# Causal attention and a token/channel mixer on one core: the 64-key ends of probabilities times values as 64x64 tiles in two PSUM banks, with a new list of places

## The chip, the cores and the metric

The kernel runs on one core of a Trainium2 chip, in float32 throughout. The metric is the device time of one execution in microseconds, as the median over several runs; lower is better. PE is the matrix engine (TensorE), DVE VectorE, ACT ScalarE, POOL GpSimd, SP the engine that issues most DMAs. PSUM, which PE alone accumulates into, has eight banks of 512 float32 columns on 128 partitions.

## What is computed

Four batches of twelve heads of causal attention over 448 positions with 64 features a head; the heads' outputs side by side form x of 448 x 768. Then two two-layer networks with residuals: over the tokens (448 to 256 to 448) and over the channels (768 to 1536 to 768).

```python
scores = scale * np.matmul(q, k.transpose(0, 1, 3, 2))     # q, k, v: (4, 12, 448, 64)
scores = np.where(mask, -1000000000.0, scores)             # mask: key after query
scores = scores - np.max(scores, axis=-1, keepdims=True)
attn = np.exp(scores)
attn = attn / (np.sum(attn, axis=-1, keepdims=True) + 1e-09)
attn_out = np.matmul(attn, v)
x = attn_out.transpose(0, 2, 1, 3).reshape(B, S, H * D)
xt = x.transpose(0, 2, 1)
h = np.maximum(xt @ w_tok1, 0.0) @ w_tok2
u = x + h.transpose(0, 2, 1)
h2 = np.maximum(u @ w_ch1, 0.0) @ w_ch2
out = u + h2
```

The weights of both networks arrive as float64.

## The kernel before

The 48 heads are worked in 24 pairs, two heads side by side on the 128 partitions. For each pair `load_pair` fetches q, k and v (`blocks` for q and k, four DMAs each; `load` for v, three), `prep` transposes q and k on DVE, and `heads` computes scores, exponentials and sums in blocks of 64 queries. The scores are matmuls on 64x64 quarters of PE's array, so that both heads and two blocks run at once. The normalized probabilities are transposed, on PE for the first ten pairs (`by_tensor`) and by DMA for the others (`by_dma`), and `values` multiplies them with the values. `xturn` transposes the result for the token network (`tokens`), two pairs at a time; `split_u`, `channels` and `group` are the channel network, and `store` and `finish` write the output. Products of the networks are done as three products of rounded parts and remainders, on the whole 128x128 array.

The code makes jobs: a function that issues a few instructions on one engine, with the jobs it needs and the buffers and banks it holds. `Plan.job` gives each job its place from the table `PLACES` (by the job's name, its rank and a count) and, where several engines could do it, the engine from `CHOICE` ("a" ACT, "d" DVE, "p" POOL). `Plan.emit` then writes the instructions: at each planned moment each free engine takes, of the jobs whose needs are planned as done and whose banks are open, the one with the lowest place. The planned durations set this order alone; on the chip every engine executes its own queue in order and waits on semaphores. Where the plan finds PE without work in the first 75 us it puts a filler matmul there (`keep_warm`, line 861), into bank 7, which the other work gets only afterwards. `SHARE` limits how many banks a kind of work holds at once; `share("a")` is for `values`.

In `values` the 448 keys are summed in blocks of 128. With causality each block of 64 queries needs full 128-key blocks and, for every second one, an end of 64 keys. `SUMS` lists, as (value block, blocks of the transposed probabilities, first query block, number of query blocks), four products with full blocks and four ends of 64 queries. The ends too are 128 keys deep: a tile `vend` holds the values of the end in the half that counts and zeros in the other, which `load_pair.lower` and `load_pair.upper` copy there for every pair (line 635 is their copy, `[64x128]` and `[64x256]`), after a clearing at the start (line 874). One of the ends, the keys from 384 on, reads `vraw` itself, whose unused part is cleared. For each entry of `SUMS` there is a matmul for each of the two heads, on the left and the right 64 columns of the array (128x64 tiles), all into one bank, in two jobs (`range(2)`, `range(2, 8)`); line 1158 is the matmul. `evac` copies the 448 columns into `u` by one instruction.

Of the kernel before, what the change touches and what calls it, by code (L numbers as in the profile page):

```python
# [21 lines left out]
    "load_pair.blocks": {-2: (2, 3), 0: (4, 5), 2: (20, 10), 4: (52, 70), 6: (138, 160), 8: (213, 238), 10: (272,  # L22
# [3 lines left out]
    "load_pair.load": {0.5: (38,), 2.5: (94,), 4.5: (113,), 6.5: (193,), 8.5: (309,), 10.5: (322,), 12.5: (389,),  # L26
        14.5: (439,), 16.5: (463,), 18.5: (577,), 20.5: (606,), 22.5: (697,), 24.5: (764,), 26.5: (846,), 28.5:
        (951,), 30.5: (1021,), 32.5: (1107,), 34.5: (1216,), 36.5: (1255,), 38.5: (1443,), 40.5: (1403,), 42.5:
        (1539,), 44.5: (1564,), 46.5: (1642,)},
    "load_pair.lower": {-0.2: (67,), 1.8: (135,), 3.8: (143,), 5.8: (220,), 7.8: (354,), 9.8: (361,), 11.8: (434,),  # L30
        13.8: (476,), 15.8: (521,), 17.8: (600,), 19.8: (643,), 21.8: (732,), 23.8: (795,), 25.8: (872,), 27.8:
        (985,), 29.8: (1047,), 31.8: (1142,), 33.8: (1243,), 35.8: (1286,), 37.8: (1467,), 39.8: (1470,), 41.8:
        (1556,), 43.8: (1599,), 45.8: (1672,)},
    "load_pair.upper": {-0.2: (72,), 1.8: (139,), 3.8: (150,), 5.8: (234,), 7.8: (364,), 9.8: (371,), 11.8: (436,),
        13.8: (489,), 15.8: (528,), 17.8: (602,), 19.8: (645,), 21.8: (701,), 23.8: (798,), 25.8: (875,), 27.8:
        (987,), 29.8: (1054,), 31.8: (1152,), 33.8: (1246,), 35.8: (1291,), 37.8: (1468,), 39.8: (1481,), 41.8:
        (1559,), 43.8: (1612,), 45.8: (1678,)},
    "narrow.load": {3.5: (107, 128, 132, 176, 187, 205, 209, 233), 12: (305,), 13: (383,), 14: (450,), 15: (484,),
        16: (591,), 17: (666,), 18: (735,), 19: (791,), 20: (855,), 21: (916,), 22: (988,), 23: (1027,), 24:
        (1099,), 25: (1173,), 26: (1266,), 27: (1328,), 28: (1381,), 29: (1434,), 30: (1472,), 31: (1524,), 32:  # L40
        (1579,), 33: (1650,), 34: (1714,), 35: (1747,)},
    "narrow.size": {3.5: (146, 162, 178, 192, 215, 231, 247, 257), 12: (346,), 13: (429,), 14: (505,), 15: (572,),
        16: (635,), 17: (716,), 18: (763,), 19: (828,), 20: (893,), 21: (949,), 22: (1008,), 23: (1072,), 24:
        (1134,), 25: (1215,), 26: (1288,), 27: (1366,), 28: (1418,), 29: (1463,), 30: (1501,), 31: (1548,), 32:
        (1619,), 33: (1694,), 34: (1737,), 35: (1766,)},
    "narrow.shift": {3.5: (153, 170, 185, 207, 218, 236, 250, 266), 12: (357,), 13: (435,), 14: (511,), 15: (542,),
        16: (644,), 17: (722,), 18: (778,), 19: (834,), 20: (898,), 21: (962,), 22: (1013,), 23: (1076,), 24:
        (1140,), 25: (1237,), 26: (1298,), 27: (1370,), 28: (1426,), 29: (1458,), 30: (1509,), 31: (1551,), 32:
        (1623,), 33: (1698,), 34: (1741,), 35: (1771,)},
    "narrow.join": {3.5: (164, 177, 199, 210, 227, 242, 256, 274), 12: (363,), 13: (437,), 14: (524,), 15: (584,),  # L50
        16: (656,), 17: (729,), 18: (783,), 19: (845,), 20: (904,), 21: (970,), 22: (1019,), 23: (1081,), 24:
        (926,), 25: (1242,), 26: (1303,), 27: (1372,), 28: (1428,), 29: (1473,), 30: (1516,), 31: (1555,), 32:
        (1626,), 33: (1702,), 34: (1308,), 35: (1776,)},
    "token_weights.<lambda>": {3.5: (168, 181, 201, 216, 232, 245, 260, 273)},
    "token_weights.rest_of": {3.5: (171, 186, 204, 219, 244, 252, 267, 280)},
    "prep.turn": {-1.5: (1, 6), 0.5: (8, 19), 2.5: (56, 59), 4.5: (96, 109), 6.5: (180, 200), 8.5: (246, 269), 10.5:
# [4 lines left out]
    "heads.<lambda>": {0: (7, 9), 2: (25, 31), 4: (66, 75), 6: (114, 118), 8: (206, 212), 10: (279, 282), 12: (333,  # L61
# [473 lines left out]
def kernel(  # L535
# [17 lines left out]
    P = 128  # L553
# [585 lines left out]
    def values(g):  # L1139
# [720 lines left out]
```

## Time and profile before

| what | us |
|---|---|
| median of three runs | 550.89 |
| lowest and highest run | 549.56, 550.93 |
| the profiled execution, its own time | 550.41 |
| its span, first to last instruction | 548.6 |
| PE busy in the span | 538.4 |
| DVE, ACT, POOL busy | 432.7, 325.0, 151.0 |

The profile is of one execution. An engine's busy time is the time in which at least one of its instructions is under way; matmuls overlap one another, so the distance between two starts tells what one costs, and its duration does not. A float32 matmul of attention appears as two passes, two instructions each of one row. L1158 and the like are lines of the kernel before.

### The profile page before, as it was taken

How to read it: one execution, taken by the hardware profiler on the slowest of the kernel's cores; microseconds unless marked ns; L12 is line 12 of the kernel's file. 1: busy time of each engine (PE TensorE's matmuls, PEld its weight loads, DVE VectorE, ACT ScalarE, POOL GpSimd, SP SyncE). 2: the span in 40 equal slices, each digit the busy share in tenths (PEclk: the TensorE clock that was granted, in tenths of full speed). 3: DMA queues.
4: the chain of work that ended last, by engine and by line, in shares of the span. 5: the costliest groups of instructions: out<-in, count | busy, mean ns of one | idle time of the engine just before them, and what ended most of it. 6: DMA issues, size and time to landing. Idle time of an engine off the chain costs nothing.

```text
span 548.6 us, 11162 instructions
## 1 busy us (share of the span) xinstructions
PE 538.4 (98%) x3908; PEld 466.3 (85%) x3908; DVE 432.7 (79%) x1052; ACT 325.0 (59%) x764; POOL 151.0 (28%) x208
## 2 busy tenths in 40 slices
PE   8998999999999999999999999999999999999996
PEld 3677788888888888888888989999999999999995
DVE  5989888888878978988787897389897857484864
ACT  4989898888795979876768872154232313140300
POOL 2536542353332132122230265161200212100000
PEclk9999999999999999999999999999999999999999
DMA  6677778899899999998987664247632121212138
GB/s 114 135 166 151 155 185 216 199 157 197 204 186 189 191 193 196 186 195 200 206 168 197 149 146 158 67 115 154 135 86 77 40 86 33 72 41 86 30 64 138
DMA packets 231783, 77.68 MB, mean 142 GB/s; under 512 B 206000, under 2 KB 221232, under 8 KB 231728
## 3 DMA queue, kind: packets, MB, share of 16 engines
q1 hardware_dynamic: 220112, 75.37, 63.9%
q10 hardware_dynamic: 11616, 1.61, 1.8%
q8 instruction: 31, 0.51, 0.4%
q14 instruction: 24, 0.20, 0.1%
HBM read 49.15 MB, written 14.94 MB: 117 GB/s over the span
## 4 chain that ended last, share of the span: by engine, by line
PE 86%; DMA 6%; SPq 4%; DVE 1%; issue 1%; ACT 1%; POOL 0%; ACTq 0%; DVEq 0%
PE ps L1328 31%; PE ps L1747 14%; PE ps L1656 12%; PE ps L1158 6%; PE ps L971 6%; PE ps L1278 5%; PE ps L1245 4%; PE ps L1727 3%; SPq L889 3%; PE ps L1062 2%; DMA out_dram<-kq 2%; DMA vraw<-in_v_dram 2%; PE ps L1197 2%; DMA gl<-in_q_dram 1%; DMA wl<-in_moe_w_tok_dram 1%
## 5 line engine op out<-in xcount | busy, mean ns | idle before, releaser
L1395 DVE TENSOR_TENSOR u<-ps,u 128x448 f32<-128x448 f32 x118 | 73.1, 621 | 43.1 <-PE ps L1747 28.4
L1005 ACT ACTIVATE prob<-prob,stat 128x128 f32<-128x128 f32 (+6 forms) x168 | 83.6, 500 | 17.5 <-DVE stat L993 17.3
L993 DVE CUSTOM_DVE_ANT_0 prob<-ps,mask 128x256 f32<-128x256 f32 (+6 forms) x168 | 63.5, 416 | 7.5 <-PE ps L971 7.1
L1328 PE MATMUL ps<-uh,wh 128*128 128x448 f32 x144 | 54.4, 378 | 0.0
L633 ACT ACTIVATE wh<-wf 128x768 fp32r<-128x768 f32 x28 | 23.3, 842 | 52.4 <-PE ps L1747 33.1
L1328 PE MATMUL ps<-gh,wh 128*128 128x448 f32 x144 | 53.9, 374 | 0.0
L635 POOL TENSOR_SCALAR prob<-prob,stat 128x320 f32<-128x320 f32 (+6 forms) x70 | 38.2, 556 | 56.6 <-DVE stat L1027 42.9
L1328 PE MATMUL ps<-uh,wl 128*128 128x448 f32 x144 | 52.7, 366 | 0.5 <-DVE wl L644 0.5
L1328 PE MATMUL ps<-gh,wl 128*128 128x448 f32 x144 | 52.7, 366 | 0.0
L1328 PE MATMUL ps<-gl,wh 128*128 128x448 f32 x144 | 52.6, 365 | 0.0
L1328 PE MATMUL ps<-ul,wh 128*128 128x448 f32 x144 | 52.6, 365 | 0.0
L644 POOL TENSOR_TENSOR wl<-wf,wh 128x768 fp32r<-128x768 f32 x17 | 32.6, 1917 | 59.4 <-ACT wh L633 57.5
L971 PE MATMUL ps<-kq,kq 64*64 64x64 f32 (+5 forms) x768 | 45.4, 360 | 0.9 <-DVE kq L938 0.9
L971 PEld LDWEIGHTS ps<-kq,kq 64*64 64x64 f32 x768 | 26.0, 132 | 19.7 <-issue 12.3
L1158 PE MATMUL ps<-pt,vraw 128*64 128x256 f32 (+2 forms) x480 | 40.4, 311 | 0.1
L639 ACT COPY pt<-pt 128x512 uint16<-128x512 uint16 (+3 forms) x45 | 38.7, 907 | 1.2 <-DMA pt<-prob 1.0
L1158 PEld LDWEIGHTS ps<-pt,vraw 128*64 128x64 f32 x480 | 28.9, 136 | 12.4 <-issue 3.2
L1005 ACT ACTIVATION_READ_ACCUMULATOR prob<-prob,stat 128x1 f32 x168 | 31.9, 190 | 0.0
L1747 PE MATMUL ps<-u,wh 128*128 128x448 f32 x108 | 30.8, 366 | 0.0
L633 ACT ACTIVATE prob<-prob,stat 128x320 f32<-128x320 f32 (+6 forms) x58 | 28.1, 510 | 2.9 <-DVE stat L1027 2.8
L1328 PEld LDWEIGHTS ps<-uh,wl 128*128 128x128 f32 x144 | 27.0, 188 | 3.1 <-DVE wl L644 0.8
L1328 PEld LDWEIGHTS ps<-uh,wh 128*128 128x128 f32 x144 | 27.1, 188 | 2.7 <-issue 0.5
(216 smaller groups left out, 1418.6 us busy)
## 6 DMA issues: line engine op xcount, KB each, us to landing
wraw<-in_moe_w_ch_dram SPq DMA_DIRECT2D x24, 768.0 KB, 5.4
wf<-scratch SPq DMA_DIRECT2D x30, 384.0 KB, 3.3
scratch<-wf SPq DMA_DIRECT2D x24, 384.0 KB, 5.6
vraw<-in_v_dram SPq DMA_DIRECT2D x48, 96.0 KB, 3.3
kq<-in_k_dram SPq DMA_DIRECT2D x60, 56.0 KB, 4.1
kq<-in_q_dram SPq DMA_DIRECT2D x56, 56.0 KB, 2.5
gh<-in_k_dram SPq DMA_DIRECT2D x36, 56.0 KB, 2.5
gl<-in_q_dram SPq DMA_DIRECT2D x36, 56.0 KB, 2.5
```

The costliest lines, as they stand in the source:

```text
L633: nc.scalar.activation(dst, src, AF.Copy, scale=scale)
L635: eng[e].tensor_scalar(dst, src, scale, 0.0, op0=ALU.mult, op1=ALU.add)
L639: nc.scalar.copy(out, in_)
L644: eng[e].tensor_tensor(dst, a, b, op=ALU.subtract)
L971: nc.tensor.matmul(scores[n].tile[lanes, to:at], lhsT=qe.tile[LANES[j], c * QC:(c + 1) * QC], rhs=ke.tile[LANES[j], slice(*keys)], start=T ...
L993: nc.vector.tensor_tensor_reduce(out=part(c, r), in0=ps.tile[:, at:at + wide(c)], in1=mask[:, S - QC:S + P] if c == 2 else mask[:, S - wid ...
L1005: nc.scalar.activation(part(c, r), part(c, r), AF.Exp, bias=stat.tile[:, 0, AT[c]:AT[c] + 1], scale=-1.0, accum_out=stat.tile[:, 1, AT[c]: ...
L1158: nc.tensor.matmul(ps.tile[LANES[j], c * QC:(c + nq) * QC], lhsT=s.tile[:, kb, j] if kb < NCH else ends.tile[:, kb - NCH, j], rhs=view[:, ...
L1328: nc.tensor.matmul(ps.tile[:, :S], lhsT=x.tile[:, at_:at_ + P], rhs=y, start=(n == 0 and i == 0), stop=(n + 1 == w[2] and i == 2),)
L1395: eng[e].tensor_tensor(u, ps.tile[:, :S], u, op=ALU.add)
L1656: nc.tensor.matmul(ps.tile[:, :S], lhsT=l()[:, t * P:(t + 1) * P], rhs=r, start=(t == 0 and n == 0), stop=(t == half - 1 and n == 2),)
L1747: nc.tensor.matmul(ps.tile[:, :S], lhsT=l.tile[:, t * P:(t + 1) * P], rhs=r.tile, start=(n == 0), stop=(n == 3 * len(fs) - 1),)
```

## The change

The four ends of `values` become products of 64 keys. `ENDS` lists them as (row half, value block, block of probabilities, query block): two read the lower 64 partitions of `vraw`, which hold their keys already, and two the upper 64 of `vend`. Each matmul now uses a 64x64 quarter of the array, and the ends of the lower and the upper row half go to two banks, `ps` and `low`. The products of query blocks 1 and 2 go to `low` as well, so that each query block lies in one bank alone. `evac` takes 256 columns from the one and 192 from the other. The copy `lower`, the zeros in `vend` and `vraw` and their clearing are dropped, and `vend` has two blocks instead of three. `values` may hold two banks.

Beside this all places in `PLACES` and the engines in `CHOICE` are new (fitted on durations with disturbances added, 2311 jobs instead of 2335), and the plan counts 1.4 us instead of 1.0 for the landing of a DMA in the first 75 us. Of the list the diff below keeps the new places of the scores (`heads.<lambda>`) and of `values.pv` and the engines of the rounding of the token weights.

```diff
--- before.py
+++ after.py
...
-    "token_weights.<lambda>": {3.5: "pppppppp"},
...
+    "heads.<lambda>": {0: (6, 9), 2: (24, 30), 4: (68, 81), 6: (112, 125), 8: (179, 190), 10: (265, 269), 12: (328,
+        335), 14: (378, 392), 16: (441, 444), 18: (505, 524), 20: (563, 575), 22: (653, 667), 24: (733, 736), 26:
+        (807, 818), 28: (880, 897), 30: (946, 962), 32: (1050, 1054), 34: (1117, 1133), 36: (1201, 1213), 38: (1285,
+        1287), 40: (1351, 1364), 42: (1423, 1426), 44: (1516, 1518), 46: (1590, 1600)},
...
+    "values.pv": {0: (99, 106), 2: (137, 146), 4: (213, 216), 6: (250, 255), 8: (342, 347), 10: (400, 405), 12:
+        (452, 458), 14: (529, 533), 16: (609, 615), 18: (659, 662), 20: (727, 740), 22: (804, 812), 24: (902, 908),
+        26: (969, 973), 28: (1045, 1048), 30: (1123, 1128), 32: (1205, 1208), 34: (1278, 1281), 36: (1355, 1359),
+        38: (1429, 1433), 40: (1521, 1526), 42: (1593, 1596), 44: (1670, 1675), 46: (1713, 1717)},
...
+    "token_weights.<lambda>": {3.5: "apapaaaa"},
...
-    LEAD, SWITCH, RING = 1400.0, 100.0, 128.0
+    LEAD, SWITCH, RING, LANDS = 1400.0, 100.0, 128.0, (1400.0, 1000.0)
...
-                    end = max(dma, end + 850.0) + 1000.0
+                    end = max(dma, end + 850.0) + (self.LANDS[0] if now < self.WARM else self.LANDS[1])
...
-    SHARE = {"s": 4, "t": 2, "a": 1, "m": 3, "w": 5}
+    SHARE = {"s": 4, "t": 2, "a": 2, "m": 3, "w": 5}
...
-    SUMS = ((0, slice(0, 4), 3, 4), (0, slice(8, 14, 5), 1, 2), (1, slice(4, 8), 3, 4), (2, slice(10, 12), 5, 2),
-            (3, slice(15, 16), 6, 1), (4, slice(15, 16), 0, 1), (5, slice(9, 10), 4, 1), (6, slice(9, 10), 2, 1))
+    SUMS = ((0, slice(0, 4), 3, 4), (0, slice(8, 14, 5), 1, 2), (1, slice(4, 8), 3, 4), (2, slice(10, 12), 5, 2))
+    ENDS = ((0, 3, 15, 6), (1, 0, 15, 0), (0, 2, 9, 4), (1, 1, 9, 2))
...
     for n in range(BUFS["vraw"]):
         keep["vraw", n] = const.tile([P, NCH, 2, D], F32, tag=f"vraw_{n}", name=f"vraw_{n}")
-        nc.gpsimd.memset(keep["vraw", n][TAIL:, NCH - 1], 0.0)
-        keep["vend", n] = const.tile([P, 3, 2, D], F32, tag=f"vend_{n}", name=f"vend_{n}")
-        nc.gpsimd.memset(keep["vend", n], 0.0)
+        keep["vend", n] = const.tile([P, 2, 2, D], F32, tag=f"vend_{n}", name=f"vend_{n}")
...
-                def lower(e, s=s, ends=ends):
-                    copy(e, kept(ends)[:QC, 1], s.tile[:QC, 2])
-
                 def upper(e, s=s, ends=ends):
-                    copy(e, ends.tile[QC:, ::2], s.tile[:QC, :2])
-
-                a = plan.job({"act": act_sb(P), "dve": dve2(P), "pool": pool1(P)}, lower, js, [s, ends], 2.0 * g + RV - 0.2, lock=True)
+                    copy(e, kept(ends)[QC:], s.tile[:QC, :2])
+
                 c = plan.job(
-                    {"act": act_sb(2 * P), "dve": dve2(2 * P), "pool": pool1(2 * P)}, upper, [a], [s, ends],
+                    {"act": act_sb(2 * P), "dve": dve2(2 * P), "pool": pool1(2 * P)}, upper, js, [s, ends],
                     2.0 * g + RV - 0.2, lock=True,
                 )
-                raws[g, nm] = s, js + [a, c], ends
+                raws[g, nm] = s, js + [c], ends
...
-        ps = share("a")
+        ps, low = share("a"), share("a")
         pt, pdone = turned.pop(g)
         if t == 0:
             utile[b] = slot("u")
         u = utile[b]
         prev = None
-        for part in (range(2), range(2, 8)):
+        for part in (range(2), range(2, 4)):
             def pv(e, part=part):
                 if part[0] == 0:
                     bank(ps)
+                    bank(low)
                 view = pt.tile.rearrange("p o (j q) -> p o j q", j=2)
                 for n in part:
                     kb, o, c, nq = SUMS[n]
                     for j in range(2):
                         nc.tensor.matmul(
-                            ps.tile[LANES[j], c * QC:(c + nq) * QC],
-                            lhsT=s.tile[:, kb, j] if kb < NCH else ends.tile[:, kb - NCH, j],
-                            rhs=view[:, o, 1 - j if c in MIXED else j],
-                            start=(n == 0),
-                            stop=(n == 7),
+                            (low if c == 1 else ps).tile[LANES[j], c * QC:(c + nq) * QC],
+                            lhsT=s.tile[:, kb, j], rhs=view[:, o, 1 - j if c in MIXED else j],
+                            start=(n < 2), stop=False,
                         )
-
-            cost = sum(10.0 + QC * SUMS[n][-1] / 0.6 for n in part) + (140.0 if part[0] else 0.0)
-            prev = plan.job({"pe": cost}, pv, js + pdone + [prev], [ps, s, ends, pt, u], rank, tiled=True)
+                for half, kb, o, c in ENDS if part[0] else ():
+                    for j in range(2):
+                        nc.tensor.matmul(
+                            (low if half else ps).tile[LANES[j], c * QC:(c + 1) * QC],
+                            lhsT=(ends if half else s).tile[LANES[half], kb, j],
+                            rhs=view[LANES[half], o, 1 - j if c in MIXED else j],
+                            start=False, stop=(o == 9),
+                        )
+
+            cost = sum(10.0 + QC * SUMS[n][-1] / 0.6 for n in part)
+            cost += 420.0 if part[0] else 0.0
+            prev = plan.job({"pe": cost}, pv, js + pdone + [prev], [ps, low, s, ends, pt, u], rank, tiled=True)
 
         def evac(e):
             if t == 0:
                 make(u, [P, NT, S], F32)
-            copy(e, u.tile[:, t], ps.tile[:, :S])
+            copy(e, u.tile[:, t, 3 * QC:], ps.tile[:, 3 * QC:S])
+            copy(e, u.tile[:, t, :3 * QC], low.tile[:, :3 * QC])
 
         first = [u_ready[b, 0]] if t else []
-        u_ready[b, t] = plan.job({"act": act_ps(S), "dve": dve1(S)}, evac, [prev] + first, [ps, u], rank)
+        u_ready[b, t] = plan.job(
+            {"act": act_ps(S) + 65.0, "dve": dve1(S) + 70.0}, evac, [prev] + first, [ps, low, u], rank
+        )
```

## Rows read from the trace of the kernel before

**Rows 1.** The page: busy us, share of the span, instructions of each engine.

```profile
PE 538.4 (98%) x3908; PEld 466.3 (85%) x3908; DVE 432.7 (79%) x1052; ACT 325.0 (59%) x764; POOL 151.0 (28%) x208
```

**Rows 2.** Stretches: length, busy us (instructions) of PE, PEld, DVE, ACT, POOL, clock, DMA.

```profile
15.00:66.00 51.00, 48.05 (x565) 37.44 (x564) 44.73 (x165) 45.45 (x146) 28.32 (x54) 1.00 0.75 155
66.00:331.00 265.00, 264.55 (x2192) 227.35 (x2190) 226.70 (x604) 212.97 (x500) 81.44 (x111) 1.00 0.90 188
331.00:541.00 210.00, 210.00 (x1045) 193.04 (x1041) 150.21 (x242) 57.60 (x91) 36.58 (x25) 1.00 0.34 83
```

**Rows 3.** PE's waits (us, times, longest): 15 to 66 us, then 66 to 541 us.

```profile
PE ps L1062 <- POOL prob L635: 2.8, 2, 2.0
...
PE ps L1328 <- DVE wl L644: 0.5, 1, 0.5
```

**Rows 4.** Fillers: the group in 15 to 66 us (count, busy us, mean ns); three on PE's timeline.

```profile
L861 PE MATMUL ps<-mask 128*128 128x512 bf16 x9 | 2.9, 379 | 0.0
...
23.98 0.81 PE L861 MATMUL ps<-mask 128*128 128x512 bf16 x3
```

**Rows 5.** PE's timeline around one job of values, and the sixth job: start, length, operation.

```profile
199.79 0.36 PE L1328 MATMUL ps<-gl,wh 128*128 128x448 f32 x1
199.99 0.37 PE L1328 MATMUL ps<-gh,wl 128*128 128x448 f32 x1
200.29 1.64 PE L1158 MATMUL ps<-pt,vraw 128*64 128x256 f32 x20
201.76 0.52 PE L1158 MATMUL ps<-pt,vend 128*64 128x64 f32 x12
...
61.52 1.64 PE L1158 MATMUL ps<-pt,vraw 128*64 128x256 f32 x20
```

**Rows 6.** The same in slices under 0.1 us: the last steps, then the scores and weight loads.

```profile
201.99 0.29 PE L1158 MATMUL ps<-pt,vend 128*64 128x64 f32 x4
...
202.05 0.23 PE L1158 MATMUL ps<-pt,vend 128*64 128x64 f32 x2
202.21 0.59 PE L971 MATMUL ps<-kq,kq 64*64 64x448 f32 x4
...
202.20 0.21 PEld L971 LDWEIGHTS ps<-kq,kq 64*64 64x64 f32 x8
```

**Rows 7.** Groups by line and shape: evacuations on ACT and DVE, count, busy us, mean ns.

```profile
L1253 ACT ACTIVATE h1h<-ps 128x256 fp32r<-128x256 f32 x24 | 9.0, 376 | 6.5 <-PE ps L1245 6.4
L633 ACT ACTIVATE u<-ps 128x448 f32<-128x448 f32 x16 | 8.6, 535 | 9.3 <-PE ps L1158 9.1
...
L1258 DVE SCALAR_TENSOR_TENSOR h1l<-ps,h1h 128x256 fp32r<-128x256 f32 x24 | 9.9, 413 | 4.4 <-ACT h1h L1253 4.3
L635 DVE TENSOR_SCALAR u<-ps 128x448 f32<-128x448 f32 x8 | 4.9, 613 | 0.7 <-PE ps L1158 0.6
```

**Rows 8.** The same view: the copies that are dropped, and the clearing on POOL.

```profile
L633 ACT ACTIVATE vend<-vraw 64x128 f32<-64x128 f32 x8 | 2.4, 303 | 0.5 <-DMA vraw<-in_v_dram 0.5
...
L635 DVE TENSOR_SCALAR vend<-vraw 64x128 f32<-64x128 f32 x7 | 1.5, 213 | 2.3 <-DMA vraw<-in_v_dram 2.3
...
L635 POOL TENSOR_SCALAR vend<-vraw 64x128 f32<-64x128 f32 x9 | 3.7, 412 | 11.1 <-DMA vraw<-in_v_dram 10.9
...
L874 POOL MEMSET vend<- 128x384 f32 x2 | 0.8, 420 | 0.1
```

**Rows 9.** Timelines of the end: first output transposes on DVE, last product on PE.

```profile
527.26 1.17 DVE L1797 STREAM_TRANSPOSE kq<-u 128x448 f32<-128x448 f32 x2
...
542.64 0.37 PE L1747 MATMUL ps<-gh,pt 128*128 128x448 f32 x1
```

**Rows 10.** The chain that ended last, in order of time: start, length, what.

```profile
530.91 1.18 DVE kq L1797 x2
...
542.54 2.43 DMA out_dram<-kq
...
545.19 0.42 DVE kq L635
```

More of the change, by code (lines that the diff above doesn't have):

```diff
@@ new lines @@
+    "load_pair.upper": {-0.2: (94,), 1.8: (129,), 3.8: (201,), 5.8: (245,), 7.8: (333,), 9.8: (377,), 11.8: (429,),
+        13.8: (470,), 15.8: (519,), 17.8: (572,), 19.8: (655,), 21.8: (716,), 23.8: (809,), 25.8: (865,), 27.8:
+        (1029,), 29.8: (1037,), 31.8: (1118,), 33.8: (1223,), 35.8: (1314,), 37.8: (1346,), 39.8: (1401,), 41.8:
+        (1512,), 43.8: (1573,), 45.8: (1646,)},
+    "narrow.load": {3.5: (83, 109, 88, 152, 175, 198, 203, 223), 12: (277,), 13: (376,), 14: (447,), 15: (509,), 16:
+        (600,), 17: (669,), 18: (725,), 19: (791,), 20: (863,), 21: (940,), 22: (1022,), 23: (1057,), 24: (1121,),
+        25: (1183,), 26: (1251,), 27: (1320,), 28: (1395,), 29: (1443,), 30: (1503,), 31: (1552,), 32: (1602,), 33:
+        (1661,), 34: (1694,), 35: (1735,)},
@@ new lines @@
+    "heads.recip": {0: (25, 49), 2: (59, 73), 4: (101, 119), 6: (149, 187), 8: (226, 272), 10: (318, 330), 12: (396,
[3 rows of a table added]
+    "by_tensor.norm": {0: (31, 27, 28, 54, 58, 53, 52), 2: (66, 65, 62, 79, 75, 76, 84), 4: (104, 103, 114, 121,
[3 rows of a table added]
+    "by_tensor.flip": {0: (36, 40, 63, 72), 2: (77, 89, 92, 118), 4: (122, 141, 156, 166), 6: (170, 185, 207, 225),
+        8: (278, 295, 305, 324), 10: (354, 357, 375, 385), 12: (411, 425, 436, 439), 14: (468, 480, 493, 503), 16:
+        (546, 552, 568, 571), 18: (581, 593, 603, 642)},
@@ new lines @@
+    "combined.sum_.do": {-4.94: (1894, 1898, 1902, 1906), -4.93: (1985, 1988, 1992, 1995), -4.92: (2045, 2047, 2048,
+        2052), -4.91: (2111, 2114, 2115, 2118), -4.9: (2175, 2178, 2184, 2189)},
+    "group.product.do": {55.44: (1895,), 55.71: (1904,), 55.98: (1917,), 56.25: (1909,), 56.52: (1935,), 56.79:
[5 rows of a table added]
+    "group.first.do": {-6: (1926, 1975, 2043, 2109, 2174)},
+    "group.plus.do": {-6: (1928, 1934, 1931, 1944, 1948, 1937, 1970, 2017, 2020, 2026, 2028, 2032, 2031, 2035, 2087,
+        2090, 2089, 2092, 2094, 2106, 2103, 2156, 2158, 2159, 2163, 2167, 2164, 2171, 2205, 2206, 2210, 2222, 2223,
+        2236, 2227)},
@@ L247 @@
+    "spared.hi": {-4.9: (2202, 2248)},
+    "spared.lo": {-4.9: (2204, 2249)},
+    "finish.plus": {-6: (2296, 2295, 2301, 2298)},
+    "finish.turn": {-6: (2297, 2299, 2305, 2303)},
+    "finish.evac": {-6: (2300, 2302, 2307, 2308)},
+    "finish.send": {-6: (2304, 2306, 2309, 2310)},
 }
 CHOICE = {
[6 rows of a table removed]
-    "token_weights.<lambda>": {3.5: "pppppppp"},
-    "token_weights.rest_of": {3.5: "ddppddpp"},
-    "heads.guard": {0: "pp", 2: "da", 4: "pd", 6: "pa", 8: "ap", 10: "dp", 12: "pp", 14: "pp", 16: "dp", 18: "ad",
-        20: "ap", 22: "pp", 24: "da", 26: "dd", 28: "pp", 30: "pd", 32: "ad", 34: "ap", 36: "ap", 38: "ad", 40:
-        "da", 42: "pd", 44: "dd", 46: "pa"},
@@ new lines @@
+    "token_weights.<lambda>": {3.5: "apapaaaa"},
+    "token_weights.rest_of": {3.5: "ppppdppd"},
+    "heads.guard": {0: "dp", 2: "pp", 4: "pp", 6: "pp", 8: "pa", 10: "ap", 12: "pp", 14: "pa", 16: "ap", 18: "aa",
+        20: "ad", 22: "ad", 24: "da", 26: "ap", 28: "pa", 30: "ad", 32: "dd", 34: "pd", 36: "pp", 38: "dd", 40:
+        "dp", 42: "ap", 44: "pp", 46: "dp"},
+    "by_tensor.norm": {0: "apdaadp", 2: "dappapp", 4: "dpapddd", 6: "appppaa", 8: "dapppap", 10: "aappapa", 12:
+        "papppap", 14: "ppapdpa", 16: "ddppaap", 18: "pppaaad"},
```

252 lines of the change are left out of this document (109 added, 143 removed), and 221 rows, old and new, of tables (CHOICE, PLACES).

## The prediction

> **What bounds the kernel now.** I read the page's busy shares first, then the stretches, then what TensorE waits for, and only then single instructions. The shares say TensorE: 538.4 of 548.6 us [rows 1]. A share alone can mislead, so the stretches come next [rows 2]. From 66 to 331 us, where attention and the feed-forward products are mixed, PE is busy for 264.55 of 265 us, and from 331 to 541 us, after the last attention product, for all of 210. From 15 to 66 us it is busy for 48.05 of 51 us. The list of PE's waits says how little is left to win there: 0.5 us between 66 and 541 us, and 2.8 us, in two pieces, between 15 and 66 us [rows 3]. In the first 66 us some of the busy time is filler that keeps the clock up and computes nothing, nine matmuls after 15 us; three in a row take 0.81 us where one takes 0.38, so a further one costs 0.215 us, and the nine hold 1.9 us [rows 4]. Beside PE, in 66 to 331 us, DVE is busy for 226.70 and ACT for 212.97 of 265 us [rows 2]: close behind, but behind. At the end it is different. The last matmul of a product starts at 542.64 us [rows 9], and the last of the output copies starts only at 545.19, behind an output DMA that began at 542.54 [rows 10]; the span ends at 548.6. So three things can move the time: what PE executes, what the first 66 us lose, and the last 6 us.
>
> **The ends as 64x64 tiles.** Per pair of heads there are 24 jobs of probabilities times values. I take the one at 200.29 us apart [rows 5]. Each matmul runs as two passes, and the two heads run beside each other in two 128x64 halves of the array, so one step of two passes serves both heads. The last 64-column ends start at 201.76 (12 passes, 6 steps), and the last step starts at 202.05 [rows 6]: 0.29 us over five steps, 0.058 us a step. One more such step pair, the end that reads vraw, lies just ahead of them, so the four ends are 8 steps, 8 x 0.058 = 0.464 us. After the change each of the four ends uses one half of the rows; two ends times two heads fill all four quarters, so 4 steps are left. That four quarters do run together is seen in the scores that follow: their eight weight loads (two passes for four quarters) are over within 0.21 us of 202.20, and four matmuls are under way from 202.21 [rows 6]. Gain per job: 4 x 0.058 = 0.232 us; 24 jobs: 5.57 us.
>
> Against it stands a change of tile shape that wasn't there: from 128x64 to 64x64 in the middle of the job. The trace prices it. Inside a run of 448-column matmuls the starts are 0.20 us apart (199.79, 199.99), and across the change to 128x64 0.30 (199.99 to 200.29) [rows 5]. From 128x64 to 64x64, the very pair in question, the step is 0.16 us (202.05 to 202.21) against 0.06 (201.99 to 202.05) [rows 6]. Both give 0.10 us. It is not paid where scores follow directly, since they are 64x64 already and would have changed shape anyway. Sorting PE's jobs by the place numbers of the new list, 10 of the 24 jobs have scores directly behind them; 14 pay: 14 x 0.10 = 1.40 us. By the same sorting the old list has 106 changes of shape and the new one 101 without the new kind, so 5 x 0.10 = 0.50 us is saved by regrouping. PE's work changes by -5.57 + 1.40 - 0.50 = -4.67 us.
>
> The Trainium skill, TensorEngine Tiling (Array Packing), section Key Properties, says that changing the tiling mode drains TensorE. The trace agrees only in part: 202.05 to 202.21 is shorter than the 0.23 us that the last step is shown to take [rows 6]. Were a full drain due, each new change would cost 0.23 - 0.06 = 0.17 instead of 0.10 us, 14 x 0.07 = 1.0 us more, and the sum below would come to -3.1.
>
> How much of the 4.67 us reaches the end: 18 of the 24 jobs run after 66 us (the sixth begins at 61.52 us [rows 5]), where PE waits for nothing, so 18/24 x 4.67 = 3.5 us does. Of the six before, ACT and DVE stand almost as full as PE (45.45 and 44.73 of 51 us [rows 2]), so I count half of 1.2 us: 0.6. Together -4.1 us; bounds -3.5 and -4.7.
>
> **The evacuation.** One read of 448 columns becomes two, of 256 and 192, out of two banks. On ACT 448 columns take 535 ns and 256 take 376 ns [rows 7], so a column costs 0.83 ns, 192 columns 323 ns, and the pair 699: +0.16 us. On DVE 613 and 413 ns give 1.04 a column, 346 for 192, and 759: +0.15 us (the 256-column row there is another operation; it is the nearest). 24 x 0.155 = 3.7 us more, divided between ACT and DVE. What is dropped is the copy of 64x128, 24 of them: 8 x 303, 9 x 412 and 7 x 213 ns [rows 8], 7.6 us on three engines, and two clears of 0.42 us on POOL at the start. The balance is about nothing for ACT and DVE. I cost both at zero on the path: what hides them is PE's queue, which waits for neither. If that cover were gone, 0.155 us a job would show, 3.7 us.
>
> **The second bank.** Each job now takes two PSUM banks at its start and holds them to the end of the evacuation. The trace of before shows no wait of PE for a bank, so I bound it: below by 0, and above by the time of one evacuation, 0.54 to 0.61 us, for each job whose bank is still being read [rows 7]. I take 0.5 us in all, as PE's waits after 66 us are 0.5 us now [rows 3].
>
> **The list.** All places and many choices of engine are new, so every step of every queue may move. In the stretch from 66 to 541 us a list can win almost nothing, as PE neither waits nor runs filler. In 15 to 66 us it can win at most 1.9 us of filler and 2.8 us of waits, 4.7, and lose an unknown amount. SP's order of the loads is nearly the old one (blocks for the eighth pair one step earlier, values of the fifth two steps earlier, of the sixth one step later). Rounding of the token weights goes from POOL to ACT for six of eight pieces, at about 0.4 us (376 ns for 256 columns [rows 7]) 2.4 us on an engine that has 5.5 us to spare there. I take 0 for this stretch, with bounds of 3 us either way.
>
> At the end I can read the order. The old list puts the first two output transposes after the third of the twelve last products, at 527.26 us [rows 9], the next pair at 530.91, and from there the chain is output DMA after output DMA [rows 10]. The new one lets the first output go after the first product, some 3.6 us earlier, and puts the fourth output, the one the chain runs through, directly behind its product instead of second in the pair of 1.18 us [rows 10]: some 0.6 us earlier. I take -0.6 us, bounds 0 and -1.2 (the last copies would then wait for PE alone).
>
> **Sum.** -4.1 + 0 + 0.5 + 0 - 0.6 = -4.2 us. The profiled execution took 550.41 us (span 548.6 and 1.8 around it), so 546.2. It lay 0.5 us under the median of the runs, 550.89, and the forecast is for the median: 546.7 us. Its own range, from the bounds: -4.7 - 1.2 - 1.8 for the better half of the list to -3.5 + 1.5 for the worse, 543.2 to 549.0.
>
> **Rivals.** (a) ACT holds up the first 66 us. The 2.4 us of rounding that comes to ACT delays the exponentials by so much, and PE with them, and the six early jobs give nothing: -3.5 + 2.4 + 0.5 - 0.6 = -1.2, 549.7 us. For it: ACT's 89% there; against: the new list takes part of the normalizations from other places and drops copies. (b) The bank: the job's first matmul stands at the head of PE's queue until a second bank is read out, and everything behind it on PE stands too. At 0.58 us a job it decides from 8 of the 24 jobs on (8 x 0.58 = 4.6 eats the gain of PE); with 18 it costs 10.4, and the time is 550.89 - 4.1 - 0.6 + 10.4 = 556.6 us. The Trainium skill, TensorEngine Tiling (Array Packing), section Gotcha 1: PSUM Pressure, says that row tiling raises the pressure on banks, as different row tiles need different ones; no run here shows its price yet. Against (b): scores already take two banks in one step, and PE waits 0.5 us in 475. (c) The row halves don't run together: then the ends keep 8 steps and pay the change, +1.4 - 0.5 + 0.5 - 0.6 = +0.8, 551.7 us. Against it stand the four quarters in [rows 6].
>
> **Chances.** Forecast 0.67, (a) 0.16, (b) 0.13, (c) 0.04. About 0.3%, 1.65 us, is what a measurement here can tell from no change: faster means under 549.2, slower over 552.5. The forecast gives 0.67 of faster (its upper edge just stays in), and (a) lies mostly within 0.3%, with 0.02 beyond on the good side; (c) is within. So faster 0.69, same 0.18, slower 0.13. The range 543.0 to 551.2 takes in the forecast's own and (a) and leaves (b) and (c) out.
>
> **What the profile after would show.** The job of probabilities times values: 1.92 us from first start to the next job now, 1.69 where scores follow and about 1.79 elsewhere if the price holds; 1.92 to 2.02 for (c). PE's waits after 66 us stay near 0.5 us; (b) would show PE waiting for the two evacuations. The last copy starts some 1.9 us after the last product's last matmul instead of 2.55 (542.64 to 545.19). PE's filler and waits in 15 to 66 us tell whether the list won or lost there; a loss of over 3 us would make the forecast wrong whatever the tiles do.

## The result, and the profile after

The changed kernel takes 546.29 us in the median of 13 runs (544.01 to 549.00). The kernel before took 551.75 (549.56 to 553.62) in the 13 runs beside them. The ratio is 0.9889, 95% interval 0.9865 to 0.9914: 6.1 us less (4.7 to 7.4). The forecast was 546.7 us, 4.2 us less than the 550.89 us of the three runs that it started from. The profiled execution took 546.4 us, its span is 544.6, 4.0 us under that of before. Single runs of one kernel spread by 4 to 5 us, so a difference of two profiles can't be held to the 6.1 of the ratio by better than some 2 us.

The page of after, as [rows 1]:

```profile
PE 535.3 (98%) x3908; PEld 460.4 (85%) x3913; DVE 426.5 (78%) x1048; ACT 327.2 (60%) x786; POOL 147.8 (27%) x186
```

The stretches of after, as [rows 2] (length, busy us and instructions of PE, PEld, DVE, ACT, POOL, the granted clock as a share of full speed, DMA share, GB/s):

```profile
15.00:66.00 51.00, 50.43 (x577) 38.43 (x580) 47.48 (x169) 48.76 (x157) 28.66 (x52) 1.00 0.75 159
66.00:331.00 265.00, 263.12 (x2194) 222.50 (x2193) 218.84 (x598) 211.88 (x513) 77.11 (x97) 1.00 0.88 187
331.00:541.00 210.00, 209.20 (x1043) 193.36 (x1041) 150.61 (x243) 58.46 (x92) 38.63 (x23) 1.00 0.35 86
```

PE is still the bound, with 3.1 us less of busy time. In 15 to 66 us PE went from 48.05 to 50.43 us busy, and ACT from 45.45 to 48.76 [rows 2].

PE's waits in after, as [rows 3]: in 15 to 66 us, then in 66 to 541 us (us, times, longest).

```profile
PE ps L1049 <- ACT prob L626: 0.3, 1, 0.3
...
PE ps L1326 <- POOL wl L637: 1.2, 1, 1.2
PE ps L958 <- DVE u L1284: 0.5, 1, 0.5
```

2.8 us of waits in the first stretch became 0.3, and 0.5 in the rest became 1.7. None of them is a wait for an evacuation of `values`: line 626 is a copy or scaling on ACT, here of probabilities, line 637 makes the lower part of a channel weight, line 1284 adds the token network's result.

PE's timeline of after around one job of values with scores directly behind it, and one with a product behind it (start, length, operation), as [rows 5] and [rows 6]:

```profile
177.73 1.52 PE L1146 MATMUL ps<-pt,vraw 128*64 128x256 f32 x16
179.18 0.27 PE L1153 MATMUL ps<-pt,vraw 64*64 64x64 f32 x2
179.20 0.27 PE L1153 MATMUL ps<-pt,vend 64*64 64x64 f32 x2
179.29 0.22 PE L1153 MATMUL ps<-pt,vraw 64*64 64x64 f32 x2
...
179.35 0.23 PE L1153 MATMUL ps<-pt,vraw 64*64 64x64 f32 x2
...
179.41 0.23 PE L1153 MATMUL ps<-pt,vraw 64*64 64x64 f32 x2
...
179.47 0.81 PE L958 MATMUL ps<-kq,kq 64*64 64x448 f32 x5
...
160.63 1.52 PE L1146 MATMUL ps<-pt,vraw 128*64 128x256 f32 x16
...
162.31 0.23 PE L1153 MATMUL ps<-pt,vraw 64*64 64x64 f32 x2
...
162.47 0.47 PE L1326 MATMUL ps<-uh,wh 128*128 128x448 f32 x1
162.78 0.36 PE L1326 MATMUL ps<-ul,wh 128*128 128x448 f32 x1
```

The four ends are four steps, and in each the lower and the upper row half start 0.01 to 0.02 us apart. The job takes 1.74 us from its first start to the scores (179.47 - 177.73), and 1.84 where a product follows (162.47 - 160.63); it was 1.92 [rows 5]. The steps are 0.06 us apart, as costed, but the first after the change of shape takes 0.11 (179.18 to 179.29). That 0.05 us is what the forecast's price of a change missed. It shows on the other side too, and larger: from 162.47 to 162.78 is 0.31 us, where two products of 448 columns stand about 0.20 apart. With the 0.16 us from the last end to this product (162.31 to 162.47, 0.10 over a step), the change into the whole array costs 0.21 us here.

### The profile page after: what moved, and what is told of

Its sections match the earlier page's. It is cut to its first block, busy times and chain, and to the rows that moved or that the text cites. A ratio compares the mean times of both kernels' runs of the same rounds, so it can differ in the third digit from the quotient of the medians.

```text
span 544.6 us, 11173 instructions
## 1 busy us (share of the span) xinstructions
PE 535.3 (98%) x3908; PEld 460.4 (85%) x3913; DVE 426.5 (78%) x1048; ACT 327.2 (60%) x786; POOL 147.8 (27%) x186
## 4 chain that ended last, share of the span: by engine, by line
PE 87%; DMA 6%; ACT 3%; SPq 2%; DVE 1%; issue 1%; ACTq 0%; POOL 0%; DVEq 0%; POOLq 0%
PE ps L1326 29%; PE ps L1745 14%; PE ps L1654 12%; PE ps L958 7%; PE ps L1146 6%; PE ps L1243 5%; PE ps L1276 5%; PE ps L1049 3%; PE ps L1725 3%; DMA out_dram<-kq 2%; PE ps L1195 2%; DMA pt<-prob 2%; SPq L880 2%; PE ps L1153 2%; PE ps L854 1%; ACT prob L992 1%
## 5 line engine op out<-in xcount | busy, mean ns | idle before, releaser
L992 ACT ACTIVATE prob<-prob,stat 128x256 f32<-128x256 f32 (+6 forms) x168 | 83.6, 501 | 12.5 <-DVE stat L980 12.2
L637 POOL TENSOR_TENSOR wl<-wf,wh 128x768 fp32r<-128x768 f32 x22 | 41.4, 1883 | 99.1 <-ACT wh L626 71.4
L980 DVE CUSTOM_DVE_ANT_0 prob<-ps,mask 128x128 f32<-128x128 f32 (+6 forms) x168 | 63.2, 414 | 4.9 <-PE ps L958 4.5
L628 POOL TENSOR_SCALAR prob<-prob,stat 128x384 f32<-128x384 f32 (+6 forms) x62 | 35.5, 580 | 60.5 <-DVE stat L1014 46.8
L958 PE MATMUL ps<-kq,kq 64*64 64x128 f32 (+5 forms) x768 | 46.6, 359 | 1.3 <-DVE stat L1011 0.8
L958 PEld LDWEIGHTS ps<-kq,kq 64*64 64x64 f32 x768 | 26.6, 133 | 20.8 <-issue 12.6
L632 ACT COPY pt<-pt 128x384 uint16<-128x384 uint16 (+3 forms) x45 | 36.1, 851 | 5.2 <-DMA pt<-prob 5.2
L1146 PE MATMUL ps<-pt,vraw 128*64 128x128 f32 (+1 forms) x384 | 37.2, 333 | 0.1
L628 POOL TENSOR_SCALAR wh<-wf 128x768 fp32r<-128x768 f32 x16 | 14.0, 876 | 70.2 <-DVE wf L696 57.2
L686 ACT ACTIVATE wf<-wraw 128x768 f32<-128x768 f32 x24 | 21.9, 911 | 17.8 <-DMA wraw<-in_moe_w_ch_dram 17.4
L632 ACT COPY prob<-prob 128x1024 uint16<-128x1024 uint16 (+1 forms) x33 | 31.0, 950 | 2.0 <-DMA pt<-prob 1.1
```

Of the source, the lines that this page charges most:

```text
L628: eng[e].tensor_scalar(dst, src, scale, 0.0, op0=ALU.mult, op1=ALU.add)
L632: nc.scalar.copy(out, in_)
L637: eng[e].tensor_tensor(dst, a, b, op=ALU.subtract)
L958: nc.tensor.matmul(scores[n].tile[lanes, to:at], lhsT=qe.tile[LANES[j], c * QC:(c + 1) * QC], rhs=ke.tile[LANES[j], slice(*keys)], start=T ...
L980: nc.vector.tensor_tensor_reduce(out=part(c, r), in0=ps.tile[:, at:at + wide(c)], in1=mask[:, S - QC:S + P] if c == 2 else mask[:, S - wid ...
L992: nc.scalar.activation(part(c, r), part(c, r), AF.Exp, bias=stat.tile[:, 0, AT[c]:AT[c] + 1], scale=-1.0, accum_out=stat.tile[:, 1, AT[c]: ...
```

## Where PE's time went

For a balance I took the distance from each matmul's start to the next. What lies above the usual distance of its shape counts as wait, fillers are kept apart, and the rest is work. Up to the start of the last product, in us:

| kernel | last product starts | filler | waits to 75 us | waits after | work | from there to the end | changes of shape |
|---|---|---|---|---|---|---|---|
| before | 542.64 | 7.62 | 6.36 | 0.62 | 526.55 | 5.99 | 103 |
| after | 538.67 | 8.00 | 4.58 | 2.59 | 522.01 | 5.94 | 118 |
| edit_old_list | 545.39 | 10.26 | 4.96 | 2.75 | 525.92 | 6.34 | 129 |
| list_old_edit | 543.13 | 11.05 | 3.99 | 0.82 | 525.78 | 5.64 | 111 |

(The rest, some 1.5 us, is the time ahead of the first matmul. Fillers and waits to 75 us are read as one sum, as some fillers left no record in a trace: after has 42 by its plan, and its trace shows 37.) After against before: work -4.54, filler and waits to 75 us -1.40, waits after 75 us +1.97, the tail -0.05; together -4.0, which is the difference of the spans.

How far one profile stands for its kernel can be read from runs below that leave the order of the work as it was. evacuation_in_two has the order of before. The largest of PE's waits in it, from 15 to 75 us and then from 75 to 541 (us, times, longest):

```profile
PE ps L1062 <- POOL prob L635: 0.4, 1, 0.4
...
PE ps L1329 <- DVE wl L644: 1.2, 3, 0.6
```

That is 0.4 us early where before has 2.8, and 2.4 us in all later where before has 0.5. row_halves_in_turn and two_more_shape_changes have the order of after; they wait 0.3 us early, as after does, and not at all later, where after has 1.7. So neither the 1.40 nor the 1.97 us can be put down to the change: waits differ by about as much between executions of one order. The spans of the runs nearest to before and after in what they execute fit the ratio better than the one pair: 549.3 (evacuation_in_two) and 547.9 (second_bank_held) against 541.8 (row_halves_in_turn) and 543.0 (last_copy_own_buffer).

## The experiments

Each ratio is to the kernel before, run beside it (medians 549.9 to 550.6 us); it isn't the quotient of the two medians. The first diff, those of the second bank, the two evacuations and the last stage are against before, the others against after, and that of old_list_less_filler against edit_old_list.

**The two parts of the change, each alone.** The first kernel has the new products, banks and evacuation with the places, engines and planning constants of before:

```diff
-    SHARE = {"s": 4, "t": 2, "a": 1, "m": 3, "w": 5}
+    SHARE = {"s": 4, "t": 2, "a": 2, "m": 3, "w": 5}
...
+    ENDS = ((0, 3, 15, 6), (1, 0, 15, 0), (0, 2, 9, 4), (1, 1, 9, 2))
...
+            copy(e, u.tile[:, t, 3 * QC:], ps.tile[:, 3 * QC:S])
+            copy(e, u.tile[:, t, :3 * QC], low.tile[:, :3 * QC])
```

> The new products, evacuation and copies with the places, engines and planning constants of the kernel before. Theory (the tiles bring most of it): 24 jobs lose 0.23 us of steps, and 16 of them, those without scores directly behind, pay a change of tile shape at 0.15 us (0.10 for the change and 0.05 that the first step after it is longer in the profile after): 5.57 - 2.4 = 3.2 us under the kernel before, ratio about 0.994. Rival (the list brings most of it): 0 to 1 us, ratio 0.998 to 1.000. Rival (the second bank costs what the tiles give where the list was not made for it): over 1.000, with PE waiting for evacuations.

The second has the products of before with the new places and engines; only the dropped copy gets a place of its own:

```diff
-    SHARE = {"s": 4, "t": 2, "a": 2, "m": 3, "w": 5}
+    SHARE = {"s": 4, "t": 2, "a": 1, "m": 3, "w": 5}
...
-        for part in (range(2), range(2, 4)):
+        for part in (range(2), range(2, 8)):
```

> The old products (128-key ends with zeros, one bank, one evacuation, both copies) with the new places, engines and landing constant; the copy that the new list has no place for stands directly ahead of the other copy of its pair, on its old engine. Theory: what is left of the change, about 2.9 us of 6.1, comes from the list: ratio about 0.995. Rival (tiles bring all): 1.000. Rival (list brings most): 0.990 to 0.992.

Measured: the edit alone 553.59 us, ratio 1.0050 (1.0027 to 1.0074); the list alone 550.66, ratio 0.9998 (0.9976 to 1.0020). Neither half of the change brings anything by itself; together they bring 1.1%. Neither is quite the half alone, though: the plan orders the jobs anew from the changed costs, banks and jobs, so neither has the exact order of before or of after, and the edit in the frozen order of before was not run. The table above says where the loss lies. With the old list the edit saves 5.57 us of steps, but it has 26 more changes of shape than before (129 to 103), which at 0.15 us each (below) take back 3.9, and those into the whole array cost more; PE's work falls by 0.6 us only. In its trace 4 of the 24 jobs have scores directly behind their ends, in that of after 10. After as a whole has 15 more changes than before. Against the 0.6 us stand 1.2 us more of fillers and waits up to 75 us, 2.1 of later waits and 0.35 of tail, together the 3.1 us by which its span is longer; the later waits alone are about what one order varies by. Fillers and waits up to 75 us are 15.2 us with the edit alone and 15.0 with the list alone, against 14.0 before and 12.6 after. The group of fillers in 15 to 66 us, of edit_old_list and then of list_old_edit (count, busy us, mean ns):

```profile
L861 PE MATMUL ps<-mask 128*128 128x512 bf16 x21 | 5.7, 379 | 0.0
```

```profile
L856 PE MATMUL ps<-mask 128*128 128x512 bf16 x24 | 6.5, 379 | 0.0
```

There were 9 in before [rows 4]. After shows 10, and row_halves_in_turn, with the same fillers and all 42 on record, 16. That led to the next question.

**Do the fillers themselves hold PE up?** The order of all jobs stays; the fillers that the plan puts after 15 us are not issued.

```diff
-                        self.filler.fn(e)
+                        if now < 15000.0:
+                            self.filler.fn(e)
```

> The kernel of edit_old_list (products and banks of the change, places and engines of before), with the same order of all jobs, but of its 50 filler matmuls the 23 that the plan puts after 15 us are left out; the filler computes nothing that is used. Theory: the 13 fillers that this kernel has more than the kernel before hold PE while real work is ready, at 0.215 us each; without all 23, up to 4.9 us of PE's queue go, and the time falls by 2.5 to 5 us, from 1.005 of the time before to 0.996 to 1.000. Rival 1: PE stands idle in the fillers' place, as the work behind them waits for DVE and ACT anyway: no change, 1.005, and PE's waits from 15 to 75 us grow by what the filler took. Rival 2: with less work on PE the granted clock of some stretch before 75 us falls below full, and the time goes up, over 1.008.

> The kernel after, with the same order of all jobs, without the 17 of its 42 filler matmuls that the plan puts after 15 us. Theory (filler holds up ready work): up to 17 x 0.215 = 3.7 us less, ratio 0.982 to 0.986. Rival 1 (PE waits in the fillers' place): 0.989 as the kernel after, with PE's waits from 15 to 66 us grown from 0.3 to some 2 us or more. Rival 2 (the granted clock falls): over 0.992, and a stretch of the first 75 us in which the granted clock is below full.

Measured: 552.29 us, ratio 1.0042 (1.0026 to 1.0058), against 1.0050 with the fillers, and 545.27 us, 0.9920 (0.9890 to 0.9951), against 0.9889. Nothing that can be measured is won in either. In after_less_filler the fillers stood where PE would wait anyway: without the 17, at 0.215 us each 3.7 us, its waits from 15 to 75 us are 4.7 us instead of 0.3. The granted clock stays at 1.00 there (2.4 GHz), so in this execution these fillers weren't needed for it either. In edit_old_list it is so in part only. In the profile of old_list_less_filler the first 75 us are 2.8 us better than in edit_old_list (12.4 us of filler and waits instead of 15.2), out of the 4.9 us of its 23 fillers, and it is given back afterwards: waits after 75 us are 4.6 us instead of 2.8, and a stretch runs at the lower clock. This execution is the slowest of its twelve (553.87 us), so it needn't be typical. Its chain of waits (start, length, what):

```profile
79.19 8.14 DMA wraw<-in_moe_w_ch_dram
...
87.41 0.89 ACT wf L694
88.30 0.46 ACT uh L634
88.77 0.50 ACT prob L634
89.27 0.28 ACT u L634
```

Its wait on PE's timeline, in brackets:

```profile
89.60 0.98 PE L966 MATMUL ps<-kq,kq 64*64 64x384 f32 x8 [1.90 <-ACT u L634]
```

And PE's stretches behind it (length, busy us, clock, DMA share, GB/s):

```profile
90.00:91.00 1.00, 1.00 (x12) 0.89 0.68 111
91.00:92.00 1.00, 1.00 (x9) 0.50 0.63 121
...
93.00:94.00 1.00, 1.00 (x18) 0.50 0.35 72
94.00:95.00 1.00, 1.00 (x12) 0.90 0.77 152
```

A weight load of 8.14 us ends late; ACT, with the load's conversion (line 694) at the head of its queue, does the copies behind it only then; PE waits 1.90 us for one of them, and from 91 to 94 us the granted clock is 0.50, 1.2 GHz. So in this execution what PE gains early runs into the loads of the weights. Whether they also set the loss of edit_old_list was not tried.

**What a change of shape costs.** Two of the four ends are put ahead of the last two full products, so that each job changes from 128x64 to 64x64 and back once more:

```diff
+                if part[0]:
+                    ends_of(ENDS[:2])
                 for n in part:
...
-                for half, kb, o, c in ENDS if part[0] else ():
+                if part[0]:
+                    ends_of(ENDS[2:])
```

> The changed kernel with the first two of its four ends ahead of the last two full-block products of the job instead of behind them: two changes of tile shape more in most of the 24 jobs, the same products. The profile after showed the first step behind a change 0.05 us longer than the others, beside the 0.10 of the change. Theory (a change costs 0.15 us in all): about 45 changes more, some 6.5 us over the changed kernel; a job is 0.30 us longer. Rival (0.10, as in the prediction): 4.5 us and 0.20. Rival (a full drain, 0.17 and the longer first step): about 9 us.

Measured: 550.27 us, ratio 1.0006 (0.9986 to 1.0026), that is 1.17% or 6.4 us more than after. Changes of shape: 161 instead of 118. The time on PE that belongs to `values`, summed over its jobs from start to start, rises from 43.76 to 50.49 us: 6.73 / 43 = 0.157 us each. The forecast's 0.10 falls, and 0.15 stands for changes between these two shapes: 0.10 from start to start and 0.05 in the step behind. PE's timeline of one job of this kernel:

```profile
179.74 0.87 PE L1158 MATMUL ps<-pt,vraw 128*64 128x256 f32 x8
180.54 0.27 PE L1146 MATMUL ps<-pt,vraw 64*64 64x64 f32 x2
...
180.64 0.23 PE L1146 MATMUL ps<-pt,vraw 64*64 64x64 f32 x2
...
180.81 0.87 PE L1158 MATMUL ps<-pt,vraw 128*64 128x256 f32 x8
181.61 0.27 PE L1146 MATMUL ps<-pt,vraw 64*64 64x64 f32 x2
...
181.78 0.56 PE L958 MATMUL ps<-kq,kq 64*64 64x448 f32 x4
```

2.04 us from the first start to the scores, where after has 1.74, for two changes more.

**Do the row halves run together only in the order of the change?** The two lower halves come first, then the two upper ones, so that neighbours in the program use the same rows.

```diff
-    ENDS = ((0, 3, 15, 6), (1, 0, 15, 0), (0, 2, 9, 4), (1, 1, 9, 2))
+    ENDS = ((0, 3, 15, 6), (0, 2, 9, 4), (1, 0, 15, 0), (1, 1, 9, 2))
```

> The changed kernel with its four ends in another order: both ends of the lower row half first, then both of the upper. Nothing else is altered. Theory (the gain is that the two row halves run side by side, and PE issues in order): a job becomes three or four steps of 0.058 us longer, 0.17 to 0.23 us, 4 to 5.5 us in all, most of the change's gain. Rival (each quarter has a queue of its own and the order doesn't matter): same as the changed kernel.

Measured: 543.77 us, ratio 0.9888 (0.9829 to 0.9947): as after. PE's timeline of one job shows why:

```profile
178.48 0.27 PE L1153 MATMUL ps<-pt,vraw 64*64 64x64 f32 x2
178.51 0.27 PE L1153 MATMUL ps<-pt,vend 64*64 64x64 f32 x2
178.59 0.22 PE L1153 MATMUL ps<-pt,vraw 64*64 64x64 f32 x2
178.62 0.23 PE L1153 MATMUL ps<-pt,vend 64*64 64x64 f32 x2
```

The program has all matmuls of the lower half ahead of those of the upper, and still the two run in step, 0.03 us apart. So the order of the four in the kernel's text needs no care here.

**The second bank and the two evacuations.** On the kernel before, each job of values takes a second bank and holds it unused until its evacuation is done:

```diff
...
-        ps = share("a")
+        ps, held = share("a"), share("a")
...
```

> The kernel before, in which each job of probabilities times values takes a second bank and holds it to the end of its evacuation without using it; its list and everything else as before, apart from the order that follows from the plan's banks. Theory (with the old list the second bank is what turned the gain of the tiles into a loss): 2 to 3 us over the kernel before, ratio 1.004 to 1.006, with more fillers in the first 75 us. Rival (banks are not short): the same as before within 0.3%, and the loss of the edit on the old list has to be looked for in its changes of shape.

And on the kernel before, one bank is read out by two instructions:

```diff
-            copy(e, u.tile[:, t], ps.tile[:, :S])
+            copy(e, u.tile[:, t, 3 * QC:], ps.tile[:, 3 * QC:S])
+            copy(e, u.tile[:, t, :3 * QC], ps.tile[:, :3 * QC])
```

> The kernel before with the one read of 448 columns out of its bank as two reads of 256 and 192. Theory (hidden behind PE's queue, as the prediction costs it): the same as before within 0.3%. Rival (the price shows): 24 x 0.155 = 3.7 us more, ratio 1.007.

Measured: 549.44 us, ratio 0.9981 (0.9959 to 1.0004), and 550.14 us, ratio 1.0003 (0.9982 to 1.0025). Neither costs anything that can be measured. The first tests what one bank less does to the other work; no instruction of the job touches the held bank, and the order of PE's work hardly moves (104 changes of shape against 103). That PE doesn't wait for the second bank's evacuation is shown by the waits of after. The groups of evacuation_in_two (count, busy us, mean ns):

```profile
L633 ACT ACTIVATE u<-ps 128x256 f32<-128x256 f32 x16 | 6.0, 374 | 5.3 <-PE ps L1158 5.2
...
L633 ACT ACTIVATE u<-ps 128x192 f32<-128x192 f32 x16 | 5.2, 322 | 0.0
...
L635 DVE TENSOR_SCALAR u<-ps 128x256 f32<-128x256 f32 x8 | 3.3, 412 | 0.6 <-PE ps L1158 0.6
...
L635 DVE TENSOR_SCALAR u<-ps 128x192 f32<-128x192 f32 x8 | 2.8, 346 | 0.0
```

376 and 323 ns on ACT, 413 and 346 on DVE had been worked out from [rows 7]: the price was right to 2 ns, and it is hidden.

**The end.** The last copy gets a buffer of its own instead of one that an output DMA still reads:

```diff
-            pt, o = share("t"), slot("kq")
+            pt, o = share("t"), slot("fin" if (b, part) == (B - 1, 1) else "kq")
```

> The changed kernel, with the last of the four output copies in a buffer of its own instead of one of the ring of five that the output transposes use. Theory (the tail waits for that buffer): the copy starts some 0.8 to 1.0 us earlier after the last product, 1.5 instead of 2.42 us after its last matmul starts, and the end comes so much earlier, ratio to the kernel before about 0.987 against 0.989. Rival (the output DMAs are the limit): the copy starts earlier but its DMA lands no earlier, same as the changed kernel.

Measured: 544.65 us, ratio 0.9880 (0.9841 to 0.9919), as after. The chain that ended last, first of after, then of this kernel (start, length, what):

```profile
532.27 2.58 DMA out_dram<-kq
...
538.43 2.43 DMA out_dram<-kq
...
541.09 0.42 DVE kq L628
```

```profile
537.81 0.40 DVE u L1767
538.21 0.04 issue
538.25 0.74 PE ps L1773 x4
539.00 0.14 issue
539.13 0.38 ACT kq L626
```

In after the last copy still stands behind a chain of output DMAs. With the buffer the chain is PE's alone, the last copy starts 1.73 us after the last product (537.40 to 539.13) instead of 2.42, and the tail is 5.63 us instead of 5.94: 0.3 us by this pair of profiles, not 1.2, and by the times nothing that can be measured.

**The last stage.** On the code of before, the 452 jobs after about 375 us get the order of the new list, and 15 of them its engine; everything ahead is untouched. Of the edit one row of places:

```diff
-    "finish.turn": {-6: (2320, 2322, 2328, 2330)},
+ 'finish.turn': {-6: (2321, 2323, 2329, 2327)},
```

> The kernel before, unchanged in its code, with the order and engines of the new list for the last stage alone (452 jobs after about 375 us) and the old list up to there. In both kernels with the old list the 448-column products of the last stage start 206.7 ns apart from 444 to 522 us, in the four with the new list 202.7. Theory (the order of the jobs decides it): 202.7 ns in that stretch, some 1.5 us under the kernel before, ratio 0.997. Rival (something upstream or the chip decides): 206.7 stays, ratio 1.000.

Measured: 547.78 us, ratio 0.9981 (0.9961 to 1.0000); the interval holds the theory's 0.997 as well as 1.000, so the time doesn't decide. What it was to test is how far apart the last stage's products of 448 columns start. Stretch 450 to 510 us, in which PE runs nearly only these: length, busy us and number of matmuls, clock, DMA share, GB/s; in turn before, after, last_stage_of_new_list and evacuation_in_two.

```profile
450.00:510.00 60.00, 60.00 (x292) 1.00 0.21 60
```

```profile
450.00:510.00 60.00, 60.00 (x298) 1.00 0.18 57
```

```profile
450.00:510.00 60.00, 60.00 (x297) 1.00 0.19 60
```

```profile
450.00:510.00 60.00, 60.00 (x298) 1.00 0.19 60
```

At full clock and without a wait, before runs 292 matmuls in these 60 us and after 298. From start to start it is 206.7 and 202.7 ns. In before it is 206 or 207 nearly every time from about 444 to 522 us, and so it is with edit_old_list, old_list_less_filler and second_bank_held; some 380 matmuls by 4 ns make 1.5 us. With the new order of the last stage it is gone. But evacuation_in_two has the old order and 298 as well, so the order isn't the cause by itself. With one profile of each kernel it isn't known either whether the step belongs to a kernel or to an execution. What makes the products fall into the slower step stays open.

## Why the prediction held, and where its steps didn't

The median, 546.29, lies 0.4 us from the forecast, and the forecast's case, PE's work at the bound, is the one that happened. That the two times lie so close is partly luck: the forecast counted from 550.89, and the runs beside the change have 551.75. As a change, its sum of -4.2 stands against -6.1 (-4.7 to -7.4) by the ratio, just outside the interval, and -4.0 in the one pair of profiles; what lies between these two can't be placed with one profile of each. Term by term the forecast was less good than its sum. (Two slips of its arithmetic change nothing: with 1.0 us more for a full drain its sum comes to -3.2, not -3.1, and its range takes +1.5 and -1.8 us for the list, where it had given the list 3 us either way.)

- **Steps, -5.57 us.** Four steps of 0.06 us are left in each job, and the row halves start together. Right; row_halves_in_turn and the job's length both bear it out, and rival (c) falls.
- **Price of a change of shape, 0.10 us.** Mis-sized. It is 0.15: the forecast priced the distance between two starts and left out that the step behind is longer too. The job therefore takes 1.74 and 1.84 us, not 1.69 and 1.79. The Trainium skill, TensorEngine Tiling (Array Packing), section Key Properties, says that changing the tiling mode drains TensorE. The trace doesn't show the full drain of 0.17 us from start to start that the prediction made of it: there it is 0.10 to 0.11 (180.64 to 180.81 in two_more_shape_changes, less a step of 0.06), as forecast. The total of 0.15 to 0.157 comes near to 0.17 only by the step behind.
- **Number of changes, 14 new and 5 fewer.** Wrong in its second half. In the trace of after 10 of the 24 jobs have scores directly behind them and 14 pay, as forecast. But the traces have 103 changes in before and 118 in after, so 104 without the new kind: 1 more, and not 5 fewer. With 0.15 each, the term is 15 x 0.15 = +2.25 us, where the forecast has +0.90.
- **PE's work, -4.67.** -4.54 in the trace, but by two errors that cancel, which is luck: the changes cost 1.35 us more, and the closer steps of the last stage, which the forecast didn't have, gave back about 1.5 in this pair of profiles.
- **How much reaches the end, -4.1, and the list in the first 66 us, 0.** Not settled by the profiles. The forecast let half of the six early jobs' gain go to waits; in the pair, filler and waits up to 75 us fell by 1.40 us, and 1.97 us more of waits came after 75 us, where the forecast has only the bank's 0.5. Both are about what waits differ by between runs of one order, so whether the list wins early and loses later isn't shown; the early sum is within the forecast's 3 us. Rival (a) falls: ACT has 3.3 us more to do in 15 to 66 us, and PE's waits there went from 2.8 to 0.3 us.
- **The list as a term of its own.** This is the step that the experiments contradict most. The sum adds the edit and the list as if each could be had alone. The edit alone is 0.5% slower, the list alone changes nothing, and both together give 1.1%. Shown of it are the numbers of changes (129 with the edit alone, 111 with the list alone, 118 with both), the 4 and 10 jobs with scores behind them, and, in one profile each, the fillers and waits of the first 75 us (15.2, 15.0, 12.6). Why PE runs out of ready work earlier with one half of the change than with both isn't settled.
- **Evacuation, 0, and second bank, +0.5.** Right: no wait on an evacuation of `values` in after, and both edits cost nothing that can be measured on the kernel before. Rival (b) falls. The Trainium skill, TensorEngine Tiling (Array Packing), section Gotcha 1: PSUM Pressure, says that row tiling raises the pressure on banks. No price of it can be measured here: the ratio is 0.9981 (0.9959 to 1.0004) with the second bank held.
- **The tail, -0.6.** Mis-sized. The last copy starts 2.42 us after the last product instead of 2.55, not 1.9. The chain of output DMAs begins its last link 0.24 us ahead of the last product (538.43, 538.67), and it was 0.10 us ahead in before (542.54, 542.64): the earlier outputs bought 0.14 us. Between single profiles the tail varies by half a us: 5.99 to 6.50 in the five with the old list, 5.57 to 6.21 in the six with the new list and its own buffers; the means differ by 0.4. So something of it may be there, though the pair before and after shows 0.05.

## What to carry to other kernels

Price a change of tile shape as the longer distance between the starts and the longer step behind it, and count the changes in a trace, not in a list of priorities: here 0.15 us each took back 40% of what the smaller tiles save. An order that was fitted to one set of operations and the operations themselves are one change; testing each half alone says what it is worth without the other, and the sum of the two is no estimate of the whole. Before a wait is put down to a change, see how much it differs in other runs with the same order. Leaving fillers out gained nothing here: in one kernel PE waited in their place, in the other the early gain was lost again.

## What the hardware showed beside this

- Products of 448 columns on the whole array, with PE never waiting and the clock granted in full, start either 202.7 or 206.7 ns apart for nearly 80 us on end, in before and evacuation_in_two with the same order of work on PE. It is worth 1.5 us here, and its cause is open.
- Quarters of the array kept pace by themselves in row_halves_in_turn: matmuls that the kernel lists half by half ran side by side, 0.03 us apart.
- A change of tile shape cost 0.15 us between 128x64 and 64x64, and 0.21 us from 64x64 into products of 448 columns on the whole array (160.63 us in after).
- In old_list_less_filler PE waited for 1.90 us up to 89.60 us; the granted clock then was 0.89, 0.50, 0.50, 0.50 and 0.90 in the five us from 90 to 95, though PE was busy in all of them. That is 1.7 us of full-speed work lost (the mean is 0.66), nearly as much again as the wait.
